# Block-recurrent attention and routed experts on one core: token values kept and written by 128 tokens, another order of the attention steps, w1 by rows 4p+k

## The chip, the cores and the metric

The kernel runs on one core of one Trainium2 chip. The metric is the device time in microseconds of that core; the time before is the median of 3 runs. Engines are named as the profile names them: PE is TensorE (PEld its weight loads), DVE is VectorE, ACT is ScalarE, POOL is GpSimd and SP is SyncE, which here only issues DMAs. A name with a q behind it (SPq, POOLq) is an engine's instruction queue.

## The reference: what is computed

Two blocks one after the other, all in fp32. The first is a cross attention in both directions between 512 tokens and 32 states for each of 8 batches and 8 heads (width 64):

```python
scores = scale * np.matmul(x, state.transpose(0, 1, 3, 2))    # x (8,8,512,64), state (8,8,32,64)
a = softmax(scores);   xread = np.matmul(a, state)            # each token reads the states
scores2 = scale * np.matmul(state, x.transpose(0, 1, 3, 2))
a2 = softmax(scores2); sread = np.matmul(a2, x)               # each state reads the tokens
x = concat([xread, sread], axis=2) -> (B, 544, 512)           # heads side by side: rows of 512
```

The second block sends each of the 8 x 544 = 4352 rows to one of 8 experts and applies that expert:

```python
logits = x @ w_gate
local_gate = sigmoid(x @ w_local)
e = argmax(logits[b, s]) if s == 0 or local_gate[b, s] < 0.5 else prev_e    # along the sequence
out[b, s] = softmax(logits[b, s])[e] * (relu(x[b, s] @ w1[e]) @ w2[e])      # w1 512x1024, w2 1024x512
```

## The kernel before

The kernel has three stages: attention, routing and experts. Instructions are issued to the engines in the order in which the program writes them (the schedule is manual): each engine, and SP with its DMAs, works through its own list in order.

**Attention.** A batch `b` is treated in small steps, each one a method of `Attention`; the string `STEPS` (L150) lists some 400 of them by a two-letter name and indices, and `reads()` (L229) issues them in that order. The order is written out by hand there, for all eight batches interleaved, and so fixes every engine's list. The steps that matter here:

- SP: `xt` loads half of a batch's transposed tokens (512 KB), `xn` its tokens (1 MB), `ws` writes the 32 finished states of a batch to the DRAM tensor `rows`, `wr` writes its finished tokens there. `xp` keeps three batches of loaded tokens.
- PE: `sc` scores, `tu` turns the exponents of the state direction, `sr` the states' reads (needs `xn`), `sl` and `lg` the logits of states and tokens, `vv` (L421) the token reads of 128 tokens. The results of all but `sc` go through four PSUM banks `p` that are used in turn.
- ACT: `et` and `ex` exponents, `ec` and `st` copies out of PSUM, `xr` (L428) the copy of a `vv` result from PSUM to SBUF, in the order of the row's columns.
- DVE and POOL: maxima, 32x32 transposes, sums and reciprocals, subtractions and multiplications of the softmax.

`xr` fills one quarter of a tile of a whole batch, 128 x (4 x 512) fp32 or 1 MB; there are three such tiles. `wr` (L434) writes one whole batch, so it waits for four `xr`, and the fourth batch's first `xr` waits until the first batch's `wr` has ended. `go` in `STEPS` hands back to the routing, and the routing calls `reads()` between its own steps to go on; some `vv`, `xr` and `wr` are done there.

**Routing** (`Routing.route`, L521). A serial chain, mostly on DVE: `choose` (L507) takes the argmax, PE turns `top`, a scan along the sequence (`run`, L549) carries the expert on, PE turns it back, prefix sums give each token its slot. Then one-hots: `inb` (L677) of a token's block of 128 slots, `inps` and `inp0` of its position in the block. `slotted` multiplies them on PE, 40 matmuls, which gives the token of each slot: first for the two first blocks only (`few`, giving `two`), then for all (`who`, giving `tok` and, through four matmuls at L715, `row`). `keep(n)` issues n matmuls whose result is not used (16 at L628, 2 at L706).

**Experts** (`experts`, L760 on). Tokens are taken in pairs of 128 of one expert. `load` fetches weights through SP; `gather_first` (L804) gathers the two first blocks of token rows by `two`, a row of 2 KB per token, and `turned(0)` turns them with PE (L836); later blocks are gathered in quarter rows of 512 bytes (`quarter`, L798) and turned by DVE in 32x32 blocks (L828; L871 for the small remainder tiles). Pair 0 is multiplied by `plain` (L1074), later pairs by a Strassen scheme with sums of the weights on DVE (`add`, L915). The first load of w1 is split in a way of its own, so that its rows stand in plain order, 16 transfers of 128 KB each to 32 partitions:

```python
            if u == 0 and i == 0:
                chunks = w1[bass.ds(e, 1), half].rearrange("o (q x) (k f) -> (o x) k q f", q=Q, k=KT)
                for j in range(KT):
                    nc.sync.dma_start(out=to[SQ * j:SQ * j + SQ], in_=chunks[:, j, 2 * other:2 * other + 2])
```

Results are scattered to the output by GpSimd.

Of the kernel before, what the change touches and what calls it, by code (L numbers as in the profile page):

```python
# [8 lines left out]
F32 = mybir.dt.float32  # L9
I32 = mybir.dt.int32  # L10
BF16 = mybir.dt.bfloat16
Act = mybir.ActivationFunctionType
Alu = mybir.AluOpType
# [5 lines left out]
P = 128  # L19
B, H, S, N, DH = 8, 8, 512, 32, 64  # L20
D = H * DH
E, F = 8, 1024
T = S + N
# [126 lines left out]
STEPS = """  # L150
sc0 kp3 xt10 xt11 mx01 ga kp2 sd0 mx00 tr01 xn0 nb0 et01 mo01 et00 tr00 tu01 sb01 gl tu00 mo00 ec01 xt20 iv0 sc1
sb00 ex01 ec00 zh01 ex00 xt31 mx11 sd1 zs01 sr0 zh00 mx10 xt21 sd3 zs00 nb1 zi0 tr11 et10 ml00 xn1 mo11 et11
tu10 ml01 tb00 st0 tu11 tr10 sd2 sb11 sc2 tb01 xt40 ec11 rt0 lg0 mo10 ex11 sl0 mx21 ec10 sb10 xt30 mx20 vv00
zh11 lt0 ex10 sk0 tr20 sr1 xn2 xr00 zh10 zs11 mo20 vv01 nb2 et21 zs10 sb20 zi1 vv03 et20 tr21 ml10 xt50 tu21
mo21 ex20 sc3 xr03 iv1 sb21 tb10 xt41 st1 iv2 xr01 tu20 rt1 ml11 mx30 ec21 sl1 xt61 mx31 ec20 vv02 zh20 ex21
tb11 sr2 nb3 zs20 xt51 zh21 et30 sk1 tr30 lg1 et31 zs21 xn3 zi2 vv11 st2 lt1 ml20 mo30 xr02 sc4 xr11 rt2 tr31
sb30 vv13 tb20 xt70 ml21 mo31 ex30 vv12 xr13 mx40 zh30 sl2 tb21 ws0 xr12 tu31 sb31 sk2 xn4 zs30 lg2 tr41 ec31
vv23 ex31 lt2 mx41 zh31 vv10 tr40 xr23 nb4 zs31 tu30 et40 xt71 zi3 vv22 mo41 ml31 et41 mo40 xt60 vv21 ec30 ml30
tb31 xr10 sc5 iv3 xr21 xn5 iv4 sb40 tb30 xr22 sr3 mx51 sb41 ex40 tr50 lg3 st3 mx50 zh40 vv31 ex41 ws3 lt3 nb5
rt3 zh41 zs40 et51 sl3 ws2 mo50 vv20 et50 xn6 sk3 zs41 sb50 zi4 tu40 xr31 tr51 sc6 xr20 ml40 mo51 ec40 tu50 ex50  # L160
ml41 tb40 ws1 tu41 ec50 mx60 vv32 zh50 wr0 ec41 tb41 sb51 sr4 zs50 xr32 mx61 ex51 tr60 lg4 nb6 et60 mo60 vv42
zh51 wr1 et61 lt4 sb60 vv43 zs51 zi5 st4 tr61 xr42 sc7 ml50 xr43 mo61 ex60 ml51 tu61 tb50 ws4 vv40 mx70 ec61 xn7
zh60 tb51 vv33 sb61 xr40 tr70 lg5 xr33 mo70 tu60 ex61 mx71 sb70 tu51 wr2 ec60 zs60 vv30 rt4 ec51 lt5 zh61 tr71
ex70 sr5 nb7 xr30 mo71 zh70 et71 sr6 zs61 sb71 wr3 zi6 et70 zs70 sl4 iv6 ml61 ex71 iv5 tu71 sk4 iv7 st5 zh71 st6
tb61 tu70 ec71 ml60 rt5 vv41 ws6 rt6 ec70 zs71 ws5 zi7 sr7 xr41 tb60 ml70 wr4 lg6 st7 ml71 tb70 sl6 sl5 rt7 vv52
lt6 tb71 sk6 lg7 sk5 xr52 ch0 ws7 vv50 sl7 xr50 vv51 lt7 sk7 go vv53 xr51 go xr53 vv61 wr5 vv60 xr61 go xr60
vv62 go xr62 vv72 vv63 xr72 vv71 xr63 wr6 vv70 xr71 go go xr70 go vv73 xr73 wr7
"""


class Attention:


    def __init__(self, ctx, tc, p, late, xn, xt, st, stt, wgl, wgs, lt, rows, none):
# [14 lines left out]
        self.sttc = [once.tile([P, n, KT, N], F32, name=f"sttc{i}") for i, n in enumerate((1, B - 1))]  # L189
        nc.sync.dma_start(out=self.sttc[0], in_=stt[:, :1])  # L190
        for h in range(2):
# [37 lines left out]
    def reads(self):  # L229

        do = dict(xt=self.load_t, xn=self.load_n, sc=self.scores, mx=self.maximum, nb=self.scaled, tr=self.turned,
                  zh=self.halves, mo=self.over_states, sb=self.subtract, ex=self.exponents, zs=self.sums,
                  zi=self.inverses, ml=self.shares, tb=self.turn_back, et=self.exponents_over_tokens, tu=self.turn,
                  ec=self.turned_to, iv=self.invert, sr=self.state_reads, st=self.states_to, rt=self.states_turned,
                  ws=self.states_to_rows, sl=self.state_logits, sk=self.state_logits_kept, lg=self.logits,
                  lt=self.logits_turned, vv=self.token_reads, xr=self.reads_kept, wr=self.reads_to_rows,
                  sd=self.diagonal, ga=self.gates, gl=self.gates_kept, ch=self.choose, kp=self.keep)
        while self.steps:
            name, at = self.steps.pop(0)
            if name == "go":  # L240
                return
            do[name](*at)
# [48 lines left out]
    def gates_kept(self):  # L291
        for u, w in enumerate(self.ws):
            self.nc.scalar.copy(self.gl[:, :, u, :E + 1], w[:, :B * (E + 1)].rearrange("p (b e) -> p b e", b=B))

    def scores(self, b):
# [132 lines left out]
    def reads_kept(self, b, c):  # L428
        xr = self.new(self.late, "xr", (b,), [P, SC, D], bufs=3)
        v = self.get("v", b, c)  # L430
        self.nc.scalar.copy(xr[:, c].rearrange("p (k u d) -> p u k d", k=KT, u=G),
                            v.rearrange("p (u k d) -> p u k d", u=G, k=KT))

    def reads_to_rows(self, b):  # L434
        if b == 0:
            self.nc.sync.dma_start(out=self.rows[NT:].rearrange("o q x -> o (q x)"), in_=self.none)
        self.nc.sync.dma_start(out=self.rows[b * T:b * T + S].rearrange("(c p) q x -> p c (q x)", p=P),
                               in_=self.get("xr", b))


class Routing:
# [79 lines left out]
    def route(self, bank, lt, slots, reads, rows):  # L521
# [105 lines left out]
        reads()  # L627
        keep(16)  # L628

# [37 lines left out]
        for c in range(n):  # L667
# [6 lines left out]
        nc.vector.tensor_tensor(bf[:, 0], inf, over(cols, 2), op=Alu.mult)  # L674
        nc.vector.tensor_scalar(bf[:, 1], inf, part, None, Alu.mult)
        inb = rt.tile([P, NG, NBLK, CG], BF16, name="inb")
        nc.vector.tensor_tensor(inb, each(place[:, :NBLK]), over(blk), op=Alu.is_equal)  # L677
# [4 lines left out]
                             Act.Copy, scale=part)  # L682
        inps = [rt.tile([P, 2, P, CG], BF16, name=f"inp{i}") for i in range(1, NG // 2)]
        for i, inp in enumerate(inps, 1):
            nc.vector.tensor_tensor(inp, each(place, 2), over(pos[:, i * n:i * n + n], P), op=Alu.is_equal)

# [18 lines left out]
        yield  # L705
        keep(2)  # L706
        nc.vector.tensor_tensor(bc[:, 0], inb, over(cols), op=Alu.mult)
# [53 lines left out]
def experts(ctx, late, tc, bank, w1, w2, rows, slots, route, routing, out):  # L761
# [20 lines left out]
    ct_ = fy.tile([P, 2, 2, FK // 2, D // 2], F32, name="ct")  # L782
    xgs_ = [fy.tile([P, 2, Q, KT, SQ], F32, name=f"xg{i}") for i in range(2)]
    xtt_ = [fy.tile([P, KT, SQ], F32, name=f"xtt{i}") for i in range(2)]
    xgt_ = [fy.tile([P, KT, SQ], F32, name=f"xgt{i}") for i in range(2)]
    tick = fy.tile([1, 1], F32, name="tick")
# [11 lines left out]
    def quarter(to, k, i):  # L798

        nc.gpsimd.indirect_dma_start(out=to.rearrange("p k t -> p (k t)"), out_offset=None,  # L800
                                     in_=rows.rearrange("n q x -> (n q) x"),
                                     in_offset=bass.IndirectOffsetOnAxis(ap=slots.row[:, k, i:i + 1], axis=0))
# [21 lines left out]
    def turned(u):  # L824
        for b in range(2):
            to = x_t[:, :, b * P:b * P + P]
            if u:
                nc.vector.transpose(to.rearrange("p k (i t) -> p k i t", i=Q),  # L828
                                    xgs_[u % 2][:, b].rearrange("p i k t -> p k i t"))
                continue  # L830

            for h, copy in enumerate((nc.vector.tensor_copy, nc.scalar.copy)):
                t = bank(P, KT * P // 2)
                for j in range(KT // 2):
                    q = slice((2 * h + j) * P, (2 * h + j + 1) * P)
                    nc.tensor.transpose(t[:, j * P:j * P + P], first[b][:, q], route.ident)  # L836
                copy(to[:, 2 * h:2 * h + 2, :], t.rearrange("p (k t) -> p k t", k=KT // 2))
# [5 lines left out]
    def load(u, i, quarters=slice(4)):  # L843

        e = index(slots.experts[0:1, u - 1:u] if u else slots.again if i else slots.expert)
        q = places(u, i)[0]
        for half, other in [((0, 0), (0, 1), (1, 0), (1, 1)), ((0, 0), (1, 0), (0, 1), (1, 1))][i][quarters]:
            to = q[half][other]
            if i:
                w = w2[bass.ds(e, 1), half, :, other]  # L850
            else:
                w = w1[bass.ds(e, 1), half, :, other * KT * F // 4:(other + 1) * KT * F // 4]
            if u == 0 and i == 0:
                chunks = w1[bass.ds(e, 1), half].rearrange("o (q x) (k f) -> (o x) k q f", q=Q, k=KT)
                for j in range(KT):
                    nc.sync.dma_start(out=to[SQ * j:SQ * j + SQ], in_=chunks[:, j, 2 * other:2 * other + 2])
            else:
                nc.sync.dma_start(out=to.rearrange("p k f -> p (k f)"), in_=w.rearrange("o p x -> (o p) x"))

    class Tile:  # L860
# [9 lines left out]
        def turned(self):  # L870
            nc.vector.transpose(self.x_t.rearrange("p k t -> p (k t)"), self.x_g.rearrange("p k t -> p (k t)"))  # L871

# [339 lines left out]
```

## Time and profile before

| | us |
|---|---|
| median of 3 runs (lowest, highest) | 561.4 (560.24, 563.32) |
| profiled execution, its own time | 561.16 |
| its span | 559.4 |
| last `choose` (argmax of the last batch) ends | 82.06 |
| last write of token values issued | 92.9 |
| first weights `a` issued | 94.16 to 103.4 |
| first expert matmul (`plain`) | 110.44 |

The profile is one execution of the program on the chip. Times in it count from the start of the span. Its timeline has one row per group of instructions: start, duration, engine, line, operation, output and inputs by the program's names, the count, and in brackets how long the engine had been idle before it and what ended that. Buffer numbers are left out, so `rows<-xr` is any write of token values. The table of stretches gives the busy time of each engine, the granted clock of TensorE as a share of full speed, the mean busy share of the 16 DMA engines, and the GB/s moved. A matmul's end is modelled, so a busy PE need not be a PE at its peak.

In the span 155.46 MB are moved, 135.84 MB of it through SP's queue (67.2% of the time of the 16 DMA engines) and 18.69 MB through GpSimd's (9.7%).

### The profile page before, as it was taken

What the parts mean: (1) busy time and instruction counts of PE and PEld (TensorE: products, weight loads), DVE (VectorE), ACT (ScalarE), POOL (GpSimd) and SP (SyncE); (2) the same over time, 40 slices, a digit from 0 to 9 for tenths busy, and PEclk for the clock granted to TensorE, in tenths of its full rate; (3) what the DMA queues carried; (4) which work ended last, traced back from release to release, by engine and by line L of the source; (5) the groups of instructions that cost most, each with busy time, mean ns of one, the idle gap of its engine ahead of it and who ended that gap; (6) DMA issues with size and microseconds to landing.
All of it is one profiled execution on the core that took longest, in us unless ns stands there. A gap on an engine that the chain in (4) does not pass through costs nothing. (4 is left out here: it accounts for less than half of the span.)

```text
span 559.4 us, 12913 instructions
## 1 busy us (share of the span) xinstructions
PE 529.4 (95%) x4905; PEld 462.4 (83%) x4905; DVE 369.0 (66%) x622; ACT 174.0 (31%) x357; POOL 300.1 (54%) x386
## 2 busy tenths in 40 slices
PE   7795987799999999999999999999999999999994
PEld 2463765698988889898989898989899999989993
DVE  6895868473847375757475647484677776678674
ACT  5883845211121223131312222222232322213230
POOL 6774730254555465646474746453764445555454
PEclk9898889599999999999999999999999999999998
DMA  8997546799998979897979898966566574846653
GB/s 311 410 373 282 168 158 248 171 342 397 360 375 283 362 284 380 300 377 286 389 289 368 306 348 330 340 222 222 166 240 219 201 259 152 291 142 244 230 191 101
DMA packets 49322, 155.46 MB, mean 278 GB/s; under 512 B 6673, under 2 KB 7825, under 8 KB 45922
## 3 DMA queue, kind: packets, MB, share of 16 engines
q1 hardware_dynamic: 41698, 135.84, 67.2%
q0 software_dynamic: 7552, 18.69, 9.7%
q8 instruction: 41, 0.67, 0.5%
q14 instruction: 31, 0.25, 0.1%
HBM read 136.68 MB, written 17.89 MB: 276 GB/s over the span
## 5 line engine op out<-in xcount | busy, mean ns | idle before, releaser
L800 POOL DMA_INDIRECT xg<-rows,row x132 | 149.9, 1136 | 29.8 <-issue 28.6
L915 DVE TENSOR_TENSOR a<-a,a 128x1024 f32<-128x1024 f32 x64 | 76.9, 1222 | 20.2 <-DMA a<-in_w_dram 18.5
L998 PE MATMUL ps<-xt,a 128*128 128x128 f32 x720 | 88.8, 276 | 0.0
L998 PE MATMUL sum<-xs,a 128*128 128x128 f32 x720 | 87.7, 275 | 0.0
L998 PEld LDWEIGHTS ps<-xt,a 128*128 128x128 f32 x720 | 84.5, 192 | 2.2 <-issue 1.8
L998 PEld LDWEIGHTS sum<-xs,a 128*128 128x128 f32 x720 | 84.0, 192 | 0.0
L915 DVE TENSOR_TENSOR c<-c,c 128x1024 f32<-128x1024 f32 x64 | 75.4, 1219 | 3.1 <-DMA c<-in_w_dram 2.4
L1038 PE MATMUL ps<-c,h 128*128 128x256 f32 x312 | 74.7, 382 | 0.0
L1038 PEld LDWEIGHTS ps<-c,h 128*128 128x128 f32 x312 | 58.0, 190 | 10.9 <-issue 3.7
L1038 PE MATMUL ps<-c,hs 128*128 128x256 f32 x256 | 60.5, 379 | 0.0
L981 POOL DMA_INDIRECT out_dram<-y,tok x32 | 34.1, 1066 | 42.6 <-DVE c L915 28.8
L1038 PEld LDWEIGHTS ps<-c,hs 128*128 128x128 f32 x256 | 48.6, 190 | 6.6
L1038 PE MATMUL sum<-c,h 128*128 128x256 f32 x200 | 47.2, 379 | 0.0
L915 DVE TENSOR_TENSOR h<-s,s 128x512 f32<-128x512 f32 x15 | 10.4, 693 | 53.2 <-ACT s L1021 36.0
L814 POOL COPY tick<-s 1x1 f32<-1x1 f32 x45 | 17.1, 379 | 49.4 <-ACT s L1021 49.1
L1038 PEld LDWEIGHTS sum<-c,h 128*128 128x128 f32 x200 | 38.0, 190 | 5.2
L949 ACT COPY sum<-ps 128x256 f32<-128x256 f32 (+1 forms) x31 | 14.3, 461 | 72.8 <-PE ps L998 53.4
L425 PE MATMUL p<-sd,a 128*128 128x256 f32 x128 | 34.3, 406 | 0.0
L1043 ACT ACTIVATE r<-sum,prob 128x256 f32<-128x256 f32 x32 | 15.2, 474 | 52.2 <-PE sum L1038 31.4
L814 POOL COPY tick<-r 1x1 f32<-1x1 f32 x41 | 11.9, 289 | 35.8 <-ACT r L1043 29.3
L1038 PE MATMUL sum<-c,hs 128*128 128x256 f32 x128 | 30.2, 379 | 0.0
L998 PE MATMUL ps<-xs,a 128*128 128x128 f32 x240 | 29.2, 275 | 0.0
(228 smaller groups left out, 752.3 us busy)
## 6 DMA issues: line engine op xcount, KB each, us to landing
c<-in_w_dram SPq DMA_DIRECT2D x68, 512.0 KB
a<-in_w_dram SPq DMA_DIRECT2D x64, 512.0 KB
at<-in_w_dram SPq DMA_DIRECT2D x18, 1024.0 KB
ct<-in_w_dram SPq DMA_DIRECT2D x18, 1024.0 KB
x_t<-in_xt_dram SPq DMA_DIRECT2D x16, 512.0 KB
x_n<-in_xn_dram SPq DMA_DIRECT2D x8, 1024.0 KB
rows<-xr SPq DMA_DIRECT2D x8, 1024.0 KB
xg<-rows,row POOLq DMA_INDIRECT x132
```

Source lines behind the costliest of these rows:

```text
L425: self.nc.tensor.matmul(v[:, d], lhsT=self.get("a", b, u)[:, c * P:c * P + P], rhs=self.sd[:, b, d], start=True, stop=True)
L800: nc.gpsimd.indirect_dma_start(out=to.rearrange("p k t -> p (k t)"), out_offset=None, in_=rows.rearrange("n q x -> (n q) x"), in_offset=ba ...
L814: nc.gpsimd.tensor_copy(tick, value)
L915: nc.vector.tensor_tensor(out, a, b, op=op)
L949: nc.scalar.copy(y, x)
L981: nc.gpsimd.indirect_dma_start(out=out, out_offset=to, in_=y, in_offset=None, bounds_check=NT - 1, oob_is_err=False)
L998: nc.tensor.matmul(to[:, m * P:m * P + P], lhsT=w[:, j, m * P:m * P + P], rhs=x[:, j, :], start=begin and m == 0 and j == 0, stop=(m == FK ...
L1038: nc.tensor.matmul(to, lhsT=x[:, m, :], rhs=w[:, m, :], start=begin and m == 0, stop=(m == FK // 2 - 1), skip_group_check=True)
L1043: nc.scalar.activation(to, t, Act.Copy, scale=p)
```

## The change

1. `xr` becomes a tile of its own for each 128 tokens (256 KB, twelve of them, as many bytes as before); `wr` writes one such tile, so there are 32 writes for 8.
2. `STEPS` is another order of the same steps, with the 32 `wr` and one step `wm14` (four matmuls with unused results before `sc1`). The first load of states goes through ACT's queue instead of SP's.
3. In DRAM, w1 is laid out so that partition p holds the rows 4p+k (k = 0 to 3). The first weights are then loaded like all others, in four transfers of 512 KB over 128 partitions. To match, the tokens are turned with a step of four columns, on PE for the first pair and on DVE for the others.
4. In the routing, the one-hots of positions (`inps`) come before those of blocks (`inb`); `keep` becomes 22 and 8 for 16 and 2.

```diff
-sc0 kp3 xt10 xt11 mx01 ga kp2 sd0 mx00 tr01 xn0 nb0 et01 mo01 et00 tr00 tu01 sb01 gl tu00 mo00 ec01 xt20 iv0 sc1
...
+sc0 kp3 xt11 xt10 mx00 ga kp2 sd3 tr01 xt21 mx01 sd2 mo01 nb0 tr00 et01 sb01 xn0 mo00 wm14 sc1 et00 sb00 ex01
...
+ex10 mx10 sc2 ml00 st0 xt30 tb01 rt0 sb11 tb00 sl0 xt31 tr20 lg0 nb1 ex11 zh10 sk0 tr21 vv03 et10 zh11 xt41 zs10
+vv00 et11 lt0 mx21 xr03 xt51 zs11 tu11 zi1 xr00 tu10 iv1 ml11 mo21 vv02 xt50 ec10 mo20 ml10 sc3 ec11 tb11 xt40
+xr02 mx20 sb21 sr1 tb10 xn2 tr30 sb20 ex21 lg1 mx30 st1 vv12 zh21 ex20 rt1 tr31 nb2 sl1 zh20 et20 vv10 zs21 sk1
+lt1 ws1 zs20 et21 tu20 zi2 xt60 mo30 xr10 ml20 sc4 xr12 iv2 mx31 ec20 xn3 ml21 tu21 tb20 vv11 mx41 ec21 nb3 sb30
+et30 tb21 sr2 tr40 et31 xt61 lg2 mo31 ex30 tu30 mo40 sb31 st2 sc5 lt2 wr00 xr11 mx40 ec30 zh30 tr41 wr03 tu31
...
+go wr50 vv43 xr51 wr51 go xr43 vv52 wr43 vv61 xr52 ws4 vv60 wr52 xr61 go ws5 xr60 vv62 wr60 go xr62 ws7 wr62
...
-        nc.sync.dma_start(out=self.sttc[0], in_=stt[:, :1])
+        nc.scalar.dma_start(out=self.sttc[0], in_=stt[:, :1])
...
+    def warmed(self, b, n):
+
+        s = self.new(self.sp, "s", (b, 0), [P, S], tag="s")
+        for i in range(n):
+            self.nc.tensor.matmul(s, lhsT=self.zero[:, :P], rhs=self.zero, start=True, stop=True)
...
-        xr = self.new(self.late, "xr", (b,), [P, SC, D], bufs=3)
+        xr = self.new(self.late, "xr", (b, c), [P, D], bufs=12)
...
-    def reads_to_rows(self, b):
-        if b == 0:
+    def reads_to_rows(self, b, c):
+        if self.none is not None:
             self.nc.sync.dma_start(out=self.rows[NT:].rearrange("o q x -> o (q x)"), in_=self.none)
-        self.nc.sync.dma_start(out=self.rows[b * T:b * T + S].rearrange("(c p) q x -> p c (q x)", p=P),
-                               in_=self.get("xr", b))
+            self.none = None
+        t = b * T + c * P
+        self.nc.sync.dma_start(out=self.rows[t:t + P].rearrange("t q x -> t (q x)"), in_=self.get("xr", b, c))
...
-        keep(16)
+        keep(22)
...
+        inps = [rt.tile([P, 2, P, CG], BF16, name=f"inp{i}") for i in range(1, NG // 2)]
+        for i, inp in enumerate(inps, 1):
+            nc.vector.tensor_tensor(inp, each(place, 2), over(pos[:, i * n:i * n + n], P), op=Alu.is_equal)
+
         inb = rt.tile([P, NG, NBLK, CG], BF16, name="inb")
         nc.vector.tensor_tensor(inb, each(place[:, :NBLK]), over(blk), op=Alu.is_equal)
...
-        keep(2)
+        keep(8)
...
-    xgs_ = [fy.tile([P, 2, Q, KT, SQ], F32, name=f"xg{i}") for i in range(2)]
+    xgs_ = [fy.tile([P, 2, Q, SQ, KT], F32, name=f"xg{i}") for i in range(2)]
...
-                                    xgs_[u % 2][:, b].rearrange("p i k t -> p k i t"))
+                                    xgs_[u % 2][:, b].rearrange("p i x k -> p k i x"))
...
-                    q = slice((2 * h + j) * P, (2 * h + j + 1) * P)
-                    nc.tensor.transpose(t[:, j * P:j * P + P], first[b][:, q], route.ident)
+                    nc.tensor.transpose(t[:, j * P:j * P + P], first[b][:, 2 * h + j::KT], route.ident)
...
-            if u == 0 and i == 0:
-                chunks = w1[bass.ds(e, 1), half].rearrange("o (q x) (k f) -> (o x) k q f", q=Q, k=KT)
-                for j in range(KT):
-                    nc.sync.dma_start(out=to[SQ * j:SQ * j + SQ], in_=chunks[:, j, 2 * other:2 * other + 2])
-            else:
-                nc.sync.dma_start(out=to.rearrange("p k f -> p (k f)"), in_=w.rearrange("o p x -> (o p) x"))
+            nc.sync.dma_start(out=to.rearrange("p k f -> p (k f)"), in_=w.rearrange("o p x -> (o p) x"))
...
-            nc.vector.transpose(self.x_t.rearrange("p k t -> p (k t)"), self.x_g.rearrange("p k t -> p (k t)"))
+            nc.vector.transpose(self.x_t, self.x_g.rearrange("p x k -> p k x"))
...
-        "w1": w1.reshape(E, Q, KT, SQ, 2, F // 2).transpose(0, 4, 1, 3, 2, 5).reshape(E, 2, P, KT * F // 2),
+        "w1": w1.reshape(E, P, KT, 2, F // 2).transpose(0, 3, 1, 2, 4).reshape(E, 2, P, KT * F // 2),
```

More of the change, by code (lines that the diff above doesn't have):

```diff
@@ L150 @@
 STEPS = """
-sc0 kp3 xt10 xt11 mx01 ga kp2 sd0 mx00 tr01 xn0 nb0 et01 mo01 et00 tr00 tu01 sb01 gl tu00 mo00 ec01 xt20 iv0 sc1
[L152 to L165, printed above, removed]
@@ L166 @@
-lt6 tb71 sk6 lg7 sk5 xr52 ch0 ws7 vv50 sl7 xr50 vv51 lt7 sk7 go vv53 xr51 go xr53 vv61 wr5 vv60 xr61 go xr60
-vv62 go xr62 vv72 vv63 xr72 vv71 xr63 wr6 vv70 xr71 go go xr70 go vv73 xr73 wr7
+sc0 kp3 xt11 xt10 mx00 ga kp2 sd3 tr01 xt21 mx01 sd2 mo01 nb0 tr00 et01 sb01 xn0 mo00 wm14 sc1 et00 sb00 ex01
+iv0 tu01 tr11 gl tu00 zh01 ex00 tr10 xt20 ec00 zh00 zs01 mo10 sd0 xn1 zs00 sb10 zi0 ec01 mx11 sd1 sr0 ml01 mo11
+ex10 mx10 sc2 ml00 st0 xt30 tb01 rt0 sb11 tb00 sl0 xt31 tr20 lg0 nb1 ex11 zh10 sk0 tr21 vv03 et10 zh11 xt41 zs10
@@ new lines @@
+vv00 et11 lt0 mx21 xr03 xt51 zs11 tu11 zi1 xr00 tu10 iv1 ml11 mo21 vv02 xt50 ec10 mo20 ml10 sc3 ec11 tb11 xt40
+xr02 mx20 sb21 sr1 tb10 xn2 tr30 sb20 ex21 lg1 mx30 st1 vv12 zh21 ex20 rt1 tr31 nb2 sl1 zh20 et20 vv10 zs21 sk1
+lt1 ws1 zs20 et21 tu20 zi2 xt60 mo30 xr10 ml20 sc4 xr12 iv2 mx31 ec20 xn3 ml21 tu21 tb20 vv11 mx41 ec21 nb3 sb30
+et30 tb21 sr2 tr40 et31 xt61 lg2 mo31 ex30 tu30 mo40 sb31 st2 sc5 lt2 wr00 xr11 mx40 ec30 zh30 tr41 wr03 tu31
+ex31 nb4 zs30 sb40 vv23 et40 mx50 xt70 ec31 mo41 tu40 zh31 ex40 rt2 sr3 sb41 zs31 ws0 xr23 zi3 xn5 et41 iv3 sl2
@@ new lines @@
+ml31 mx51 vv22 ex41 sk2 iv4 st3 ml30 tb31 sc6 xr22 rt3 ec40 zh41 tb30 xt71 sl3 zh40 zs41 lg3 tr50 nb5 vv31 wr02
+zs40 et50 zi4 vv01 xn4 lt3 xr31 ml40 mo50 sk3 tr51 xr01 vv13 ml41 tb40 et51 vv21 mo51 sb50 xr13 wr10 iv5 vv20
+tb41 xr21 sb51 xn6 mx60 ex50 lg4 mx61 xr20 zh50 tu50 ex51 lt4 tu41 tr60 nb6 ec50 zh51 tu51 zs50 et60 mo60 vv32
+wr20 ec51 zs51 sb60 zi5 tu60 ec41 wr23 tr61 sc7 xr32 ml50 wr11 ex60 mo61 sr4 et61 ml51 tb50 wr12 mx71 sr5 sb61
+ws2 st4 tb51 ec60 ws3 vv30 tr70 zh60 ex61 xn7 mx70 st5 lg5 zh61 xr30 zs60 tu61 mo70 nb7 et70 vv40 zs61 sb70 zi6
@@ new lines @@
+ec61 tu70 lt5 wr22 iv6 xr40 ml61 rt5 sr6 rt4 ex70 tr71 wr40 ec70 ml60 mo71 sl5 et71 wr13 sl4 sk5 tb61 vv41 sb71
+st6 wr31 tb60 tu71 zh70 ex71 sk4 iv7 wr32 lg6 rt6 xr41 zs70 zh71 sl6 ec71 lt6 wr21 vv42 zs71 zi7 wr01 sr7 sk6
+xr42 ml71 ch0 wr42 vv33 st7 ml70 wr41 vv50 tb71 xr33 wr33 tb70 vv53 xr50 rt7 wr30 lg7 xr53 sl7 lt7 wr53 vv51 sk7
+go wr50 vv43 xr51 wr51 go xr43 vv52 wr43 vv61 xr52 ws4 vv60 wr52 xr61 go ws5 xr60 vv62 wr60 go xr62 ws7 wr62
+vv71 wr61 vv72 xr71 wr71 vv63 xr72 wr72 vv70 xr63 go wr63 go xr70 wr70 ws6 go vv73 xr73 wr73
@@ L236, in reads @@
                   lt=self.logits_turned, vv=self.token_reads, xr=self.reads_kept, wr=self.reads_to_rows,
-                  sd=self.diagonal, ga=self.gates, gl=self.gates_kept, ch=self.choose, kp=self.keep)
+                  sd=self.diagonal, ga=self.gates, gl=self.gates_kept, ch=self.choose, kp=self.keep, wm=self.warmed)
         while self.steps:
@@ L428, in reads_kept @@
     def reads_kept(self, b, c):
-        xr = self.new(self.late, "xr", (b,), [P, SC, D], bufs=3)
+        xr = self.new(self.late, "xr", (b, c), [P, D], bufs=12)
         v = self.get("v", b, c)
-        self.nc.scalar.copy(xr[:, c].rearrange("p (k u d) -> p u k d", k=KT, u=G),
+        self.nc.scalar.copy(xr.rearrange("p (k u d) -> p u k d", k=KT, u=G),
                             v.rearrange("p (u k d) -> p u k d", u=G, k=KT))
-    def reads_to_rows(self, b):
-        if b == 0:
+    def reads_to_rows(self, b, c):
+        if self.none is not None:
             self.nc.sync.dma_start(out=self.rows[NT:].rearrange("o q x -> o (q x)"), in_=self.none)
-        self.nc.sync.dma_start(out=self.rows[b * T:b * T + S].rearrange("(c p) q x -> p c (q x)", p=P),
-                               in_=self.get("xr", b))
+            self.none = None
+        t = b * T + c * P
+        self.nc.sync.dma_start(out=self.rows[t:t + P].rearrange("t q x -> t (q x)"), in_=self.get("xr", b, c))
 class Routing:
@@ L682, in route @@
                              Act.Copy, scale=part)
-        inps = [rt.tile([P, 2, P, CG], BF16, name=f"inp{i}") for i in range(1, NG // 2)]
-        for i, inp in enumerate(inps, 1):
-            nc.vector.tensor_tensor(inp, each(place, 2), over(pos[:, i * n:i * n + n], P), op=Alu.is_equal)
         def slotted(to, x):
@@ L782, in experts @@
     ct_ = fy.tile([P, 2, 2, FK // 2, D // 2], F32, name="ct")
-    xgs_ = [fy.tile([P, 2, Q, KT, SQ], F32, name=f"xg{i}") for i in range(2)]
+    xgs_ = [fy.tile([P, 2, Q, SQ, KT], F32, name=f"xg{i}") for i in range(2)]
     xtt_ = [fy.tile([P, KT, SQ], F32, name=f"xtt{i}") for i in range(2)]
-    xgt_ = [fy.tile([P, KT, SQ], F32, name=f"xgt{i}") for i in range(2)]
+    xgt_ = [fy.tile([P, SQ, KT], F32, name=f"xgt{i}") for i in range(2)]
     tick = fy.tile([1, 1], F32, name="tick")
@@ L798, in quarter @@
     def quarter(to, k, i):
-        nc.gpsimd.indirect_dma_start(out=to.rearrange("p k t -> p (k t)"), out_offset=None,
+        nc.gpsimd.indirect_dma_start(out=to.rearrange("p x k -> p (x k)"), out_offset=None,
                                      in_=rows.rearrange("n q x -> (n q) x"),
```

## The prediction

> **What bounds the kernel now.** I read the engines' busy time and the 40 slices first, then the stretches of 2 us, the timeline around each hole, and the waits.
>
> ```profile
> span 559.4 us, 12913 instructions
> PE 529.4 (95%) x4905; PEld 462.4 (83%) x4905; DVE 369.0 (66%) x622; ACT 174.0 (31%) x357; POOL 300.1 (54%) x386
> ...
> PE   7795987799999999999999999999999999999994
> ...
> DMA  8997546799998979897979898966566574846653
> ```
>
> A slice is 14 us. From slice 9 (about 110 us) on TensorE is full: the experts run from 110.44 us to the end with some 7 us of idle. So the start of `plain`, the first expert product, sets the end one for one, and only 0 to 110 us can give much. The chain of waits shows only its last piece (GpSimd gathers from 525 us) and is no use here. In the stretches of 2 us (columns: stretch, PE, PEld, DVE, ACT, POOL, granted clock, DMA share, GB/s):
>
> ```profile
> 46.00:48.00 2.00, 2.00 (x25) 0.92 (x24) 1.85 (x5) 0.10 (x2) 2.00 (x3) 1.00 1.02 283
> 48.00:50.00 2.00, 0.31 (x3) 0.07 (x1) 1.71 (x3) 0.00 (x0) 0.78 (x1) 1.00 0.89 336
> 50.00:52.00 2.00, 0.00 (x0) 0.00 (x0) 0.00 (x0) 0.00 (x0) 0.00 (x0) 1.00 1.04 397
> 52.00:54.00 2.00, 0.00 (x0) 0.00 (x0) 0.00 (x0) 0.00 (x0) 0.00 (x0) 0.62 1.05 407
> ...
> 56.00:58.00 2.00, 2.00 (x17) 1.17 (x19) 0.77 (x2) 1.56 (x4) 1.53 (x2) 0.50 0.08 27
> ```
>
> Every engine stands while the DMA engines are full; then the clock is 0.50. The timeline says why:
>
> ```profile
> 46.57 1.28 SPq L437 DMA_DIRECT2D rows<-xr  x2
> ...
> 54.30 1.07 ACT L431 COPY xr<-p 128x512 f32<-128x512 f32 x2 [8.20 <-DMA rows<-xr]
> 54.94 0.72 PEld L370 LDWEIGHTS p<-ident,e 128*128 128x128 f32 x4 [6.87 <-ACT xr L431]
> 54.94 1.12 PE L370 MATMUL p<-ident,e 128*128 128x128 f32 x4 [6.64 <-ACT xr L431]
> ```
>
> The token values of three batches fit (`xr`, three buffers of 1 MB). `wr0` is issued only at 46.57, behind `ws3` and `xn6` on SP, though its first piece was copied at 23.69. The copy of a fourth batch waits 8.20 us for it, TensorE 6.64 us for that copy's PSUM bank. Then, at the hand-over to the experts:
>
> ```profile
> 94.16 9.22 SPq L856 DMA_DIRECT2D a<-in_w_dram  x16
> ...
> 101.44 1.11 POOL L806 DMA_INDIRECT y<-rows,two  x1 [2.16 <-ACT pb L681]
> ...
> 106.03 0.49 PE L715 MATMUL ps<-wd,turn 128*128 128x98 bf16 x4 [0.41 <-DVE wd L711]
> ...
> 109.53 1.12 PE L836 MATMUL ps<-ident,y 128*128 128x128 f32 x4 [0.49 <-DMA y<-rows,two]
> ...
> 110.44 1.94 PE L1082 MATMUL ps<-xt,a 128*128 128x128 f32 x8
> ```
>
> The first weights go out in 16 transfers until 103.4 and keep the DMA engines about full until 107.5, at 190 to 270 GB/s. The two gathers of the first tokens are queued in that traffic, and TensorE turns the second at 109.53.
>
> **The change, part by part.**
>
> *Token values by 128 tokens, earlier.* In the new order `wr00` and `wr03` stand on SP behind `xt61`, whose other conditions (sc3, st1) were met by 28 us in this trace; and the thirteenth `xr`, the first that needs a buffer back, needs `wr03`. So the stall goes: 6.64 us of TensorE. With it goes its cold restart: at clock 0.50 and just after, `tu` took 1.12 instead of 0.66, the two `vv` 1.91 instead of about 1.0, `sr` 1.85 instead of 1.10: 2.1 us. Two later holes (1.99 us of TensorE at 69.6; some 1.4 us of slow clock at 73 to 76) may go or be replaced: bounds 0 and 3.4, I take 0, as the new order must have some holes of its own. **8.7 us.**
>
> What is late next? From 21.7 to 48.3 TensorE has hardly a gap and VectorE is about 94% busy, so those two. VectorE's work from 8.4 to 82 us is 57 us, TensorE's about as much; ending by 73 us leaves 8 us for the fill and the last batch's chain. DMA: 17.8 MB of inputs and some 5 MB of writes by then, at the 380 GB/s of these stretches, 61 us. It fits.
>
> SP issues 32 writes for 8 at 0.37 us each: 9 us more. They lie in SP's own waits (24.5 us for `ys`, 23.0 for `xr`, 15.2 for scores); uncovered, each delays the loads behind it by 0.4 us. Queued behind a waiting write are `xn4`, `xn6` and `xn7`, for which TensorE's in-order `sr4`, `sr6` and `sr7` wait. By the order, `xn4` has 7 us to spare, the others some 5.
>
> A rule speaks against small writes: the Trainium skill, "DMA: Bandwidth & Descriptors", section "Bandwidth", wants 1 MiB or more in a DMA for 75% of the peak, and its fit (2.0 us plus bytes over 436 GB/s, in "Anatomy of one DMA") makes 2.6 us of 256 KB: one after another, 83 us against 35 for the eight. The row nearest is the 16 loads of 128 KB: 2 MB in 13.4 us with the gathers among them, 0.84 us each, not the 2.3 of that fit, since several are in flight. By this row the 32 writes take at most 1.7 us each, 54 us in all, beside compute from 29 us on; by the 320 to 395 GB/s at which the 1 MB writes moved at 64 to 72 us, 0.75 us each. I take the latter, as the packets stay 2 KB rows over 128 partitions. No cost.
>
> *Order, routing part.* Before the first hand-back to the routing one `vv` fewer is done (22 for 23): minus 1.0 us. It comes back between the turning of `top` and of `run`: before, two `vv` filled 82.75 to 84.74 and the scan ended at 84.59; three end at 85.7, so the chain slips 1.0. Net 0; I put 1.0 as the bound on each side. The write of the states, four warming matmuls (0.9 us, in TensorE's wait for `xn0` and scores at 13.6 to 16.1) and the first state load on ScalarE's queue (0.4 us earlier for `xt0`, 0.4 us of ScalarE before its table load, idle then): 0 to minus 0.4, I take minus 0.3.
>
> *First weights in four transfers.* SP needs 4 x 0.45 = 1.8 us instead of 9.2. At the 390 GB/s of the 512 KB loads (120 to 122 us) the 2 MB end by about 100, before the first gather is issued. A gather without company: `xgt`, issued 108.26 to 109.20, moved its bytes by 110.5. So `y` is there near 103.5 and 105. What is late next: TensorE's queue. `who` (40 matmuls until 105.6) and the four of L715 (until 106.52) stand ahead of the turning. Two turnings of 1.12 us from 106.5 end at 108.75 instead of 110.65: **1.9 us.** Their weight loads now read every fourth fp32; no row shows that. Bounds 0 and a doubling of eight loads of 0.18, 1.4 us; I take 0.3, as the matmuls beside them are longer. Net 1.6.
>
> *Block one-hots last.* `inps` (2.49 us) end 1.17 us earlier, at 98.4, `inb` at 99.5, so `two` comes 0.6 us earlier. But `y` is no longer late, so this buys nothing. `who` needs `pb`, whose ScalarE step (1.92 us) now starts at 99.55 instead of 98.64 and ends at 101.5: `who` starts at 101.6 against 101.7. Nothing, within 0.3. If the cover of `who` were gone it would be 0.6.
>
> *keep 22 and 8.* Six matmuls of 0.226 end at 97.0, before the last one-hot; eight end at 100.9, before 101.6. No cost. The clock fell to 0.50 at 100.25 and came back at 113.75; in that time the turnings cost 0.9 us more and `plain` did 12 matmuls in 2 us instead of 20, some 1.5. If the extra matmuls hold the clock, minus 2.4; if not, 0. The fall came despite TensorE's 1.47 of 2 us at 98 to 100, nearly all matmuls of 4 columns, so I take 0.
>
> *w1 by rows 4p+k.* Loads after the first keep their shape. The turnings on VectorE (32 of 0.70 us, 9 of 0.30) read with a step of four fp32. The Trainium skill, "SBUF — State Buffer", "Door 1: The DMA port swizzle", says full bandwidth needs two hits in a 16-byte line; this step makes one. It gives no price: doubling, as an estimate, is 1.4 us a pair. The nearest row is the strided reduction of L641, 0.77 us against 0.49 for the contiguous one of L732: by it 0.8 a pair. Either is hidden: TensorE starts a pair 3.3 to 5.7 us after the last sum of its columns (474.66 to 477.93 is the closest). With that cover gone it would be up to 0.8 x 16 = 13 us.
>
> **Sum**, against the profiled execution's 561.16 us (span 559.4 and 1.8 around it; the median of the runs is 561.4): 8.7 + 0.3 + 1.6 = 10.6, so 550.6; on the median, 550.8.
>
> **Rivals.** (1) *The stall is only moved* (the new order's writes and loads meet elsewhere; half is lost): 8.7 becomes 4, total 5.9, 555.5. For it: in steady state a batch needs 3 MB, 7.5 us of DMA at 400 GB/s, about what VectorE needs (7.1). (2) *The clock holds* until `plain`: minus 2.4 more, 548.4. (3) *Slower: `x_n` behind waiting writes.* SP is one queue; if a `wr` or `ws` waits for ScalarE, `xn6` and `xn7` come late, and TensorE stands at `sr6` and `sr7`. An occurrence like the old stall costs 6.6 + 2.1 = 8.7 us; it decides from 10.6 us on, so at the second: 561.4 - 10.6 + 17.4 = 568. Against it: the writes ahead are of pieces copied long before in the order. (4) *The change doesn't do what it says* (gathers still late): 1.6 lost, 552.4, inside the range of the forecast.
>
> **Chances.** Forecast (with 4) 0.54, rival 1 0.20, rival 2 0.10, rival 3 0.10, a small stall that eats nearly all 0.06. The range 547 to 559 leaves out rival 3 and the edges. A measurement of this kernel can tell about 0.5%, 2.8 us. Faster by more 0.83, within 0.07, slower 0.10.
>
> **What would show it.** Right: no wait of ScalarE `xr` for `rows<-xr`, no stretch with all engines at 0; `choose` some 9 us earlier; four `a` loads in about 2 us; `y` turned straight after L715; L828 at 0.7 to 1.4 us with TensorE full. Wrong: TensorE waiting for `x_n` or for `xr`; idle TensorE at the start of pairs; the hand-over longer than now.

## The result and the profile after

Four runs of the changed kernel took 547.97 to 548.38 us, median **548.29**; the kernel before took 560.24 to 563.32 beside them, median 562.04. The ratio is 0.9757 [0.9727, 0.9786]: 2.4% faster, 2.5 us below the forecast of 550.8. The profiled execution took 547.97 us.

The page of the changed kernel: the span, the busy time of the engines, and the slices of TensorE and of the DMA engines.

```profile
span 546.2 us, 12964 instructions
...
PE 525.4 (96%) x4921; PEld 459.2 (84%) x4921; DVE 382.4 (70%) x622; ACT 173.7 (32%) x357; POOL 318.4 (58%) x386
...
PE   7789889999999999999999999999999999999993
...
DMA  8999777699989899897979797974748484666743
```

The slice in which TensorE was half idle (slice 4) is gone, and TensorE is full from slice 7 on instead of slice 9. DVE and POOL do more than before (13.4 and 18.3 us); neither became the bound. In the stretches of 2 us where every engine stood (columns as before):

```profile
48.00:50.00 2.00, 2.00 (x25) 1.79 (x16) 2.00 (x5) 2.00 (x4) 1.65 (x3) 1.00 0.85 347
50.00:52.00 2.00, 2.00 (x27) 0.86 (x29) 1.93 (x5) 2.00 (x6) 1.51 (x2) 1.00 1.02 382
```

All engines work, at full clock, and the DMA engines are about as full as before. No `xr` waits for `rows<-xr` anywhere. At the hand-over to the experts (timeline):

```profile
84.49 1.95 SPq L861 DMA_DIRECT2D a<-in_w_dram  x4
...
92.49 0.96 POOL L815 DMA_INDIRECT y<-rows,two  x1 [0.30 <-issue]
...
96.08 0.33 PE L724 MATMUL ps<-wd,turn 128*128 128x98 bf16 x4 [0.41 <-DVE wd L720]
...
96.52 1.20 PE L844 MATMUL ps<-ident,y 128*128 128x128 f32 x8
97.79 14.56 PE L1085 MATMUL ps<-xt,a 128*128 128x128 f32 x128
```

The weights go out in 1.95 us for 9.22, the tokens of both blocks are there when TensorE has done L724, and `plain` starts at 97.79. Its 128 matmuls take 14.56 us; before they took 16.14. Put together, from the timelines of the two profiled executions:

| stretch | before | after | difference |
|---|---|---|---|
| start to the end of the last `choose` | 82.06 | 71.38 | -10.68 |
| to the first `plain` | 28.38 | 26.41 | -1.97 |
| to the first second product (L1038, L1041) | 23.38 | 21.81 | -1.57 |
| to the start of the last eight matmuls | 416.16 | 415.78 | -0.38 |
| to the end of the span | 9.4 | 10.8 | +1.4 |
| span | 559.4 | 546.2 | -13.2 |

### The profile page after: what moved, and what is told of

It reads as the page before. It is cut to its first block, busy times and chain, and to the rows that moved or that the text cites. A ratio compares the mean times of both kernels' runs of the same rounds, so it can differ in the third digit from the quotient of the medians.

```text
span 546.2 us, 12964 instructions
## 1 busy us (share of the span) xinstructions
PE 525.4 (96%) x4921; PEld 459.2 (84%) x4921; DVE 382.4 (70%) x622; ACT 173.7 (32%) x357; POOL 318.4 (58%) x386
## 5 line engine op out<-in xcount | busy, mean ns | idle before, releaser
L809 POOL DMA_INDIRECT xg<-rows,row x132 | 158.0, 1197 | 26.5 <-issue 25.6
L1041 PE MATMUL ps<-c,h 128*128 128x256 f32 x312 | 74.7, 382 | 0.0
L1041 PEld LDWEIGHTS ps<-c,h 128*128 128x128 f32 x312 | 58.0, 190 | 10.9 <-issue 3.7
L1041 PE MATMUL ps<-c,hs 128*128 128x256 f32 x256 | 60.5, 379 | 0.0
L1041 PEld LDWEIGHTS ps<-c,hs 128*128 128x128 f32 x256 | 48.6, 190 | 6.6
L1041 PE MATMUL sum<-c,h 128*128 128x256 f32 x200 | 47.2, 379 | 0.0
L1041 PEld LDWEIGHTS sum<-c,h 128*128 128x128 f32 x200 | 38.0, 190 | 5.2
L918 DVE TENSOR_TENSOR h<-s,s 128x512 f32<-128x512 f32 x15 | 10.5, 698 | 44.8 <-ACT s L1024 37.6
L823 POOL COPY tick<-r 1x1 f32<-1x1 f32 x41 | 20.7, 504 | 32.9 <-ACT r L1046 30.7
L823 POOL COPY tick<-s 1x1 f32<-1x1 f32 x45 | 18.5, 410 | 35.6 <-ACT s L1024 35.5
L837 DVE STREAM_TRANSPOSE xt<-xg 128x512 f32<-128x512 f32 x32 | 34.0, 1088 | 2.5 <-DMA xg<-rows,row 2.4
L432 PE MATMUL p<-sd,a 128*128 128x256 f32 x128 | 32.1, 390 | 0.0
L1041 PE MATMUL sum<-c,hs 128*128 128x256 f32 x128 | 30.2, 379 | 0.0
```

What stands on the lines that cost most here:

```text
L432: self.nc.tensor.matmul(v[:, d], lhsT=self.get("a", b, u)[:, c * P:c * P + P], rhs=self.sd[:, b, d], start=True, stop=True)
L809: nc.gpsimd.indirect_dma_start(out=to.rearrange("p x k -> p (x k)"), out_offset=None, in_=rows.rearrange("n q x -> (n q) x"), in_offset=ba ...
L823: nc.gpsimd.tensor_copy(tick, value)
L918: nc.vector.tensor_tensor(out, a, b, op=op)
L1041: nc.tensor.matmul(to, lhsT=x[:, m, :], rhs=w[:, m, :], start=begin and m == 0, stop=(m == FK // 2 - 1), skip_group_check=True)
```

## The experiments

Times are medians; each ratio is to the kernel before on the same chip. The single runs of one kernel lie up to 6 us apart, so for questions below 3 us I read the distances of this table instead of the medians. They come from one profiled execution of each kernel:

| kernel | median (range), us | ratio | `choose` ends | to `plain` | to second product |
|---|---|---|---|---|---|
| before + attention part | 548.05 (546.88 to 549.32) | 0.9793 [0.9751, 0.9835] | 70.94 | 27.62 | 22.33 |
| before + w1 part | 557.38 (554.56 to 558.71) | 0.9943 [0.9915, 0.9971] | 80.52 | 25.96 | 22.37 |
| before, wr0 and wr1 early | 554.83 (552.14 to 555.57) | 0.9894 [0.9849, 0.9939] | 77.20 | 28.21 | 23.53 |
| before, pieces only | 554.13 (553.03 to 557.78) | 0.9913 [0.9886, 0.9940] | 79.20 | 26.68 | 22.10 |
| before, pieces written early | 551.38 (547.39 to 553.39) | 0.9811 [0.9775, 0.9846] | 71.56 | 26.39 | 22.42 |
| after, keep 16 and 2 | 548.00 (545.31 to 549.58) | 0.9776 [0.9741, 0.9811] | 71.40 | 26.88 | 23.23 |
| after, block one-hots first | 547.94 (547.05 to 548.94) | 0.9782 [0.9751, 0.9813] | 69.78 | 27.89 | 21.81 |
| after, block one-hots first, keep 22 and 2 | 550.39 (549.09 to 552.50) | 0.9798 [0.9768, 0.9828] | 70.43 | 27.18 | 23.15 |
| after, one vv later | 547.80 (546.35 to 551.01) | 0.9787 [0.9754, 0.9820] | 70.73 | 25.52 | 21.80 |
| the same again | 546.88 (545.12 to 550.89) | 0.9739 [0.9705, 0.9773] | 70.21 | 25.54 | 21.80 |
| after, turnings twice | 546.44 (545.02 to 548.25) | 0.9770 [0.9737, 0.9802] | 69.90 | 26.40 | 21.79 |
| after, unchanged | 549.78 (546.80 to 552.57) | 0.9789 [0.9753, 0.9825] | 69.58 | 26.91 | 22.32 |

The last row is the changed kernel again: its `choose` ends 1.8 us before that of the first profile. Differences of that size in the column `choose` tell nothing.

My theory was the prediction's: the stall goes, the gathers come in time, the rest is nothing. The rivals were that the stall only moves, and that the clock holds.

**The two halves alone.** Only the attention part of the diff (items 1 and 2), and only item 3:

```diff
 # attention part                              # w1 part
+ xr tiles of 128 tokens, bufs=12             + w1 by rows 4p+k, xgs_ and x_t to match
+ new STEPS with 32 wr and wm14               + first weights by the common dma_start
+ sttc[0] through nc.scalar.dma_start         # STEPS, xr, keep and one-hots as before
```

> Before, with the attention part of the change alone (new order of steps, token values by 128 tokens, first state load on ScalarE's queue, the four warming matmuls); w1, one-hots and keep as before. If the attention stage gave what the two traces show (choose 10.7 us earlier, the turning of run 1.0 us later after it): 9.7 us faster than before, about 552. Rival, that the parts behind the attention give most of it: at most 6 us, 556 or more.

> Before, with w1 by rows 4p+k and the first weights in four transfers alone. If the gathers of the first tokens were held up by the 16 transfers: the turning right after L715, 1.6 to 2.0 us faster, 560. Rival, TensorE's queue sets the start of plain whatever the loads do: 0. If the strided turnings on VectorE were not hidden: slower by up to 13 us.

The attention part gave nearly the whole gain (11.9 us on its chip, more than the 9.7 expected); the w1 part alone 0.6% or 2.6 us, and on top of the first it can't be told from nothing in the medians. Why the second doesn't add shows at the hand-over of the attention part alone, where the first weights still go out in 16 transfers:

```profile
84.13 9.11 SPq L864 DMA_DIRECT2D a<-in_w_dram  x16
...
92.88 0.95 POOL L814 DMA_INDIRECT y<-rows,two  x1 [0.30 <-issue]
...
96.41 1.09 PE L844 MATMUL ps<-ident,y 128*128 128x128 f32 x4
97.66 1.11 PE L844 MATMUL ps<-ident,y 128*128 128x128 f32 x4 [0.16 <-DMA y<-rows,two]
```

TensorE waits 0.16 us for the gathered tokens, not 1.43 and 0.49 as before. In the kernel before, 1 MB of token values went out at 92.9, right in front of the weights; here the last write is 256 KB. By the profiles below it is the size of the writes: in the old order TensorE still waits 0.52 us for the gathered tokens with pieces alone, and 1.62 with whole batches written earlier. So either half makes the gathers nearly punctual, and their gains overlap: the w1 part took 2.4 us off the hand-over alone (28.38 to 25.96), 0.4 behind the attention part (below).

**What in the attention part does it: the time of the writes, or their size?** First the old order with whole batches, `wr0` and `wr1` moved ahead of the loads that they had stood behind; then the old order with pieces, each batch's four writes where its one write had been:

```diff
-tb31 xr10 sc5 iv3 xr21 xn5 iv4 sb40 ...         # wr0, wr1 50 and 66 steps later
+tb31 xr10 sc5 iv3 xr21 xn5 wr0 wr1 iv4 sb40 ...
```

```diff
-        xr = self.new(self.late, "xr", (b,), [P, SC, D], bufs=3)
+        xr = self.new(self.late, "xr", (b, c), [P, D], bufs=12)
-... zh50 wr0 ec41 ...
+... zh50 wr00 wr03 wr01 wr02 ec41 ...
```

> Before, only wr0 and wr1 moved in the order, from behind ws1 to directly behind xn5; still 1 MB each and three buffers. If the stall was the lateness of wr0: no wait of xr for rows at 46 to 54 us, 6.6 to 8.7 us faster, 553 to 555. Rival, it is the size of a write and of a buffer: the wait stays, or moves to wr2 at the next batch, gain under 3 us.

> Before in its old order, only the token values by 128 tokens: twelve tiles, each wr replaced on the spot by the four writes of its batch. If lateness was the cause, the pieces are issued as late as before and the wait of xr stays, one copy later and some 4 us shorter as the first piece lands sooner: gain 3 to 5 us. Rival, the size was the cause: the wait is gone, gain 7 to 9 us.

The early whole-batch writes (timeline):

```profile
48.90 1.07 ACT L430 COPY xr<-p 128x512 f32<-128x512 f32 x2 [2.05 <-DMA rows<-xr]
...
65.57 0.49 PE L402 MATMUL p<-wgs,rt 128*32 128x9 f32 x6 [2.81 <-issue]
```

The wait of `xr` falls from 8.20 to 2.05 us, but doesn't go, and part of the gain is lost in a longer hole ahead of `sl` (2.81 us for 1.99): 5.2 us faster on that chip, between the two expectations. The late pieces:

```profile
52.31 0.58 ACT L431 COPY xr<-p 128x512 f32<-128x512 f32 x1 [6.00 <-DMA rows<-xr]
52.95 2.08 PE L425 MATMUL p<-sd,a 128*128 128x256 f32 x4 [4.47 <-ACT xr L431]
```

Pieces that are issued as late as before leave most of the wait (6.00 for 8.20 us). They gain 5.9 us all the same, more than expected, but not all in this stage: in the profiles `choose` ends 2.9 us earlier, 1.7 come at the hand-over (28.38 to 26.68) and 1.3 behind it. Each of the two edits gives about 1%. Then both, in the old order: each piece written some twelve steps behind its copy.

```diff
-sr1 xn2 xr00 zh10 zs11 ... et20 tr21 ml10 ... zh50 wr00 wr03 wr01 wr02
+sr1 xn2 xr00 zh10 zs11 ... et20 tr21 wr00 ml10 ... zh50
```

> Before in its old order, token values by 128 tokens as in b_pieces, and each write twelve steps behind its copy in the order. If late writes were all that the attention stage lost: choose some 11 us earlier as in b_attn, 549 to 550. Rival, the old order has holes of its own (TensorE 2 us before sl4, the cold clock after it): no wait of xr for rows, but choose only 5 to 7 us earlier, 553 to 555.

Measured 551.38 with runs from 547.39 to 553.39, between the two expectations. In the profile, which is of its fastest run, no `xr` waits for `rows<-xr`, and `choose` ends at 71.56, within the range of the new order's (69.58 to 71.40). Its hole ahead of `sl` is 1.57 us, the new order's 1.49. So early and small writes are enough for a `choose` as early as the new order's. The new order and all the rest of the change add 1.6 us between the medians on that chip (551.38 and 549.78, ranges overlapping), which can't be told from nothing. Whole batches in the new order were not tried: it copies a piece of the fourth batch (`xr31`) before the last of the first (`xr01`), so with three whole-batch tiles it would wait for itself.

**keep and the one-hots.**

```diff
-        keep(22) ... keep(8)
+        keep(16) ... keep(2)
 # the other run, block one-hots first: inb ahead of inps again, keep 22 and 8
```

> The changed kernel with keep 16 and 2 as before instead of 22 and 8. If the ten added matmuls hold the clock: it falls to 0.50 before the turning, plain and the turning take 1.6 and 0.4 us longer, 550.3. Rival, the clock held because plain comes sooner after the one-hots: no fall, 548.3.

> The changed kernel with the block one-hots first again. If who (through ScalarE's pb) and not the gather sets plain: within 0.3 us of the changed kernel, or 0.2 faster. Rival, the gather's early issue counts: 0.6 to 1.2 us slower, about 549.

With 16 and 2 the clock falls before `plain`; in the changed kernel's first profile it does not. Two stretches of the kernel with 16 and 2, then the same two of the changed kernel (columns as before; the clock is third from the end):

```profile
90.00:92.00 2.00, 0.18 (x3) 0.29 (x4) 1.15 (x2) 1.77 (x1) 0.88 (x1) 0.81 0.89 348
98.00:100.00 2.00, 2.00 (x12) 2.00 (x11) 1.84 (x7) 0.45 (x2) 0.95 (x1) 0.50 0.00 0
```

```profile
90.00:92.00 2.00, 1.43 (x9) 0.69 (x8) 1.15 (x2) 1.76 (x1) 0.89 (x1) 1.00 0.86 326
98.00:100.00 2.00, 2.00 (x19) 2.00 (x19) 1.90 (x8) 0.12 (x1) 0.95 (x1) 1.00 0.15 33
```

`plain` does 19 matmuls in 2 us instead of 12. By the distances that is 0.47 us before `plain` and 1.42 behind it, 1.9 together. The median doesn't show it (548.00, where 550.3 was expected). Five of these profiles have the one-hots last and 22 and 8 (two of them 18 and 8): in four the clock held until `plain` and beyond. In the changed kernel run again it was lost for some 3.4 us, and its distance lies between (22.32):

```profile
94.00:96.00 2.00, 1.70 (x10) 1.53 (x10) 1.74 (x6) 0.08 (x1) 0.00 (x0) 0.59 0.00 0
96.00:98.00 2.00, 2.00 (x13) 2.00 (x11) 1.71 (x8) 0.67 (x2) 0.95 (x1) 0.55 0.00 0
```

So the ten matmuls make it likely that the clock holds, not sure.

Block one-hots first: I had expected nothing, and `plain` starts 1.5 us later behind `choose`. Its timeline shows why:

```profile
88.82 3.05 PE L538 MATMUL sum<-place,identb 128*128 128x512 bf16 x7
...
91.67 3.90 PE L700 MATMUL ps<-pb,inp 128*128 128x98 bf16 x40
```

The clock falls at about 89.4 (0.85 over 88 to 90, 0.50 over 90 to 92 us), so the `keep` take 0.43 us each instead of 0.23; and `who` stands behind them on TensorE's queue and starts as they end, waiting for nothing else. To part the two, one-hots first with `keep(2)`:

> The changed kernel with the block one-hots first, as in a_inb_first, and the second keep at 2 again (the first stays 22). If in a_inb_first the eight keep matmuls, now in front of a who that is ready, made the 1.5 us from choose to plain: that goes, who starts within 20.3 us of choose, but the clock is 0.50 at the start of plain, so the second product is 1.5 us later. Rival, the one-hots themselves held who: it starts as late as in a_inb_first, 21.9 us after choose.

`who` now starts 20.71 us after `choose` (91.14 after 70.43): 0.3 later than with the one-hots last (20.43), 1.2 earlier than with eight `keep` in front. The clock is 0.50 at the start of `plain`, and the second product comes 1.3 us later behind it (23.15 for 21.81). So the order of the one-hots is worth 0.3 us by itself, and it is what makes room for the eight `keep`.

**The third `vv` between the turnings.** `vv52`, `xr52` and `wr52` go to the very end of `STEPS`:

```diff
-... xr43 vv52 wr43 vv61 xr52 ws4 vv60 wr52 xr61 go ...   xr73 wr73
+... xr43 wr43 vv61 ws4 vv60 xr61 go ...   xr73 wr73 vv52 xr52 wr52
-        keep(22)
+        keep(18)
```

> The changed kernel with vv52, xr52 and wr52 moved from the stretch between the turnings of top and run to the very end of the steps, and keep 18 for 22. If three token reads there hold the turning of run by 1.0 us and nothing takes its place: plain 1.0 us earlier, 547.3. Rival, the later first weights (queued behind wr52) or the copy take it back: 548.3.

The scan of `run` and the turning behind it, in this kernel and then in the changed one:

```profile
72.15 1.27 DVE L556 TENSOR_TENSOR_SCAN run<-hold,ps 8x544 bf16<-8x544 bf16 x1
...
73.50 0.25 PE L560 MATMUL ps<-identb,run 8*128 8x8 bf16 x4
```

```profile
72.79 1.27 DVE L557 TENSOR_TENSOR_SCAN run<-hold,ps 8x544 bf16<-8x544 bf16 x1
...
75.01 0.25 PE L561 MATMUL ps<-identb,run 8*128 8x8 bf16 x4
```

TensorE turns `run` 0.1 us after the scan instead of 0.9, and `plain` is 0.9 us nearer to `choose`. The median couldn't show it, so it was run again beside the unchanged kernel:

> The same as a_vv52 (three token reads become two between the turnings of top and run, the third goes to the end), now beside the changed kernel on one chip: 1.0 us less than it. Rival: 0.

> The changed kernel itself again, for the runs beside it on this chip: 547.5 to 548.5, with the last choose within 69.5 to 71.5 us of its profile.

546.88 against 549.78, with overlapping ranges; the unchanged kernel itself came out above the 547.5 to 548.5 expected. The distance to `plain` is 25.54 again (26.91 in the unchanged one, where the clock fell, and 26.41 in its first profile). This is the best version that I have: 0.9739 [0.9705, 0.9773] of the kernel before. What is shown is the 0.9 us of the traces, not the 2.9 of the medians.

**The turnings on VectorE, twice for each pair:**

```diff
+                nc.vector.transpose(to..., xgs_[u % 2][:, b].rearrange("p i x k -> p i k x"))   # the same once more
```

> The changed kernel with each VectorE turning of a pair's tokens issued twice (the second repeats the first), 32 more of 1.09 us, 2.2 us in each pair. If they lie in a cover of over 2 us: within 0.5 us of 548.3, TensorE as full as before. Rival, the 0.8 us a pair that the new layout costs has used up the cover: up to 16 times some 1 to 2 us slower, 560 or more.

From the second product to the last matmuls it took 414.66 us, no more than the other kernels (414.65 to 417.48). 2.2 us more per pair are hidden as well.

## Where the prediction was right and where it failed

- **The stall** (8.7 us: 6.64 of stall, 2.1 of cold restart): right in its mechanism, as the old order with early pieces shows, and short in size. At the turning of `run` 9.0 us was forecast (the stall and 0.3 for the start); 9.66 came (84.67 to 75.01), and 11.46 in the second profile. Between 8 us and the end of `choose` TensorE was idle for 12.9 us before and 7.4 after: the stall's 6.64 went and 1.1 of other holes came, among them 1.4 us within an `sr` at 38, for which the row names no releaser, and 1.5 ahead of `sl` at 59. So the later hole of 1.99 us was replaced, as assumed. The term of the sum that was too small is the slow clock: TensorE was busy 5.2 us less (61.1 to 55.9), with one `vv` of 1.0 fewer and 1.0 of warming matmuls more. Besides the restart at 52 to 59 us, the clock before was at 0.50 in two more stretches of 3.4 us, from 18.4 and from 73.0 us. In the rows of 2 us around them:

```profile
20.00:22.00 2.00, 2.00 (x28) 0.34 (x23) 0.94 (x4) 1.88 (x5) 1.24 (x3) 0.56 1.01 397
...
74.00:76.00 2.00, 2.00 (x58) 1.43 (x60) 1.41 (x3) 0.59 (x1) 1.77 (x2) 0.50 0.06 17
```

  The forecast put the one at 73 at 1.4 us and took nothing for it, and did not name the one at 18. At half clock each costs some 1.7 us, as an estimate from TensorE's 3.4 us of work in it. The one at 73 is gone in all nine profiles of the new order. The one at 18 is no safe gain: five of the nine have it, and their `choose` ends no later (69.78 to 71.40 us, against 69.58 to 71.38 without). One row of the working is misread, to no effect on the sum: the 1.91 us at 55.85 are one `vv`, not two.
- **The start** (0.3): the first states' scores begin at 5.89 for 6.04. Too small to be told from the scatter.
- **Writes at no cost, against the rule that wants 1 MiB:** right; the page cited there gives the rule and its fit for single DMAs issued from GpSimd, and these are many, issued from SP. SP issues the 32 at 0.31 to 1.04 us each, and the DMA engines moved 432, 347 and 382 GB/s in the three stretches from 46 to 52 us. Rival 3 (`x_n` behind waiting writes) didn't come: the one wait for `x_n` is that of the first `sr`, 2.67 us for 2.55 before.
- **The order in the routing** (1.0 less before, 1.0 more between the turnings): the second half came as forecast, 2.62 to 3.63 us; taking it away gained it back.
- **First weights in four transfers** (1.9 us): the w1 part alone took 2.4 off the hand-over, about what the forecast said. But the step took the gathers' lateness as this edit's alone, and the earlier, smaller writes remove most of it too: the attention part by itself took 1.8 off the hand-over (28.38 + 1.01 for the `vv` - 27.62). Behind it the four transfers, read as the attention part against the changed kernel with the one-hots first and keep 22 and 2, are worth 0.4 (27.62 - 27.18). Together 2.2 for the 1.9 predicted: the sum held, its cause was half another.
- **Strided weight loads** (0.3 taken of 0 to 1.4): nothing. At the same granted clock of 0.50 the middle one of the eight took 227 ns before and 230 with the w1 part alone (209 in the changed kernel, at full clock).
- **Block one-hots last** (nothing, within 0.3): 0.3. What the step overlooked is its bearing on `keep`: with eight `keep` and the block one-hots first, `plain` comes 1.5 later.
- **keep 22 and 8** (0 taken of 0 to 2.4): failed. The reason given, that TensorE's 1.47 of 2 us hadn't held the clock before, counted busy time without asking of what: these were matmuls of 4 columns. With six more of 512 columns ahead of them and six more behind, it held in four profiles of five. That the ones behind do most of it is likely, not shown: it held with 18 and 8 too, and fell with 22 and 2, but there with the block one-hots first. Undoing both costs 1.9 us in the profiles. This was rival 2, given a chance of 0.10.
- **Turnings on VectorE** (0.8 a pair by the row, 1.4 by the doubling estimated from the Trainium skill, "SBUF — State Buffer", "Door 1: The DMA port swizzle"): the strided reduction was the right neighbour, at 1.55 times the contiguous duration, and the cover held, even for twice as many.

```profile
L837 DVE STREAM_TRANSPOSE xt<-xg x32: 1056/1094/1110, 129.0 to 531.0; 128x512 f32<-128x512 f32 x32
```

The middle one of 32 took 1094 ns (least, middle and most are given), before 704; two make a pair, 0.8 us.

- **Rival 1** (the stall only moved, 555.5) is out: no wait of that kind is left. What the sum didn't have is the tail: from the last matmuls to the end 10.8 us for 9.4, the last scatter waiting 2.3 us for the one before it. It was 9.4 to 9.7 us in the four kernels with the old order and the old layout, 10.5 to 11.9 in all others, those with half of the change among them; why stays open.

From the 550.6 forecast for the profiled execution to its 547.97, then: 0.7 us more from the attention, 0.3 from the gathers, 0.3 from weight loads that cost nothing, 0.3 from the one-hots, 2.0 from the clock (0.47 ahead of `plain` and 1.57 behind it) and 0.4 in the experts, against 1.4 at the tail. The largest term of the miss is the clock. That the median (548.29) stands on rival 2's 548.4 is in part chance: beside the 2.0 of the clock, the other terms add 2.0 and the tail takes 1.4.

## What to carry to other kernels

A buffer is free when its write has ended, so place the write in its queue by when the copy was done, and cut it to what one copy fills; here each of the two alone gave 1%, and both in the old order most of what the new one gave. Two edits that cure the same lateness don't add up: before summing them, ask what each leaves for the other. Extra matmuls that are to hold the clock belong into a wait of TensorE; here, in front of work that was ready and already at half clock, each cost 0.43 us instead of 0.23, and `plain` came later.

## What the runs showed of the hardware

- The granted clock fell at about 100.3 in the kernel before although no wait of TensorE in the 12 us ahead of it was longer than 2.04 us; it had done 40 matmuls of 4 columns in the last 2.6. The Trainium skill, "TensorE: Matmul & The Clock Gate", "Part 1: The HAM clock gate", speaks of about 3.4 us of idleness; read as a gap in TensorE's work, no fall was due. What goes with the fall is the time without wider matmuls, from the end of the first `keep` to the start of the second: 3.0 to 4.4 us in the nine profiles where the clock fell there, 2.04 to 2.05 in the five where it held. But in one of these five, the changed kernel run again, it fell at 94.4 us, behind 40 matmuls of 98 columns and no gap over 0.61 us since 82. So narrow matmuls may count for little, and what counts stays open; no run had them alone changed.
- The same step of four fp32 made VectorE's 32x32 turning 1.55 times as long (704 to 1094 ns) and left TensorE's weight loads as they were (227 and 230 ns at half clock).
- The same code differs from run to run: the last `choose` by 1.8 us (69.58 to 71.40), the experts by 2.8 (414.65 to 417.48) with TensorE busy throughout. No row explains either.
